# A selective-scan chunk loop on TensorE: own products head by head, one state addition, and another order of products, decay, rank, masks and scatters

## The chip, the cores and the metric

The kernel runs on one core of a Trainium2 chip. The metric is the device time of one execution in microseconds (us). The five engines of the core run their own instruction streams: TensorE (PE: matrix products, its weight loads listed apart as PEld), VectorE (DVE), ScalarE (ACT), GpSimd (POOL) and SyncE (SP, which here only issues transfers). They wait for each other through semaphores, and an instruction that waits holds back everything behind it on its own engine.

## The reference, cut to what matters

Two blocks run one after the other. The first is a state-space scan (Mamba-2) over 4 batches of 8 heads, 768 positions, head width 32 and state width 16; the second is a mixture of experts with one expert per token (3072 tokens of width 256, 8 experts, hidden width 1024).

```python
# scan; x [4,8,768,32], a [4,8,768], B and C [4,8,768,16]
log_a = np.log(np.clip(a, 1e-06, 1.0))
for c in range(nc):                                   # chunks; the result does not depend on their length
    cum = np.cumsum(la, axis=-1)
    L = np.exp(cum[:, :, :, None] - cum[:, :, None, :]) * causal
    M = np.einsum('bhin,bhjn->bhij', Cc, Bc) * L
    y_intra = np.einsum('bhij,bhjd->bhid', M, xc)
    y_inter = np.einsum('bhin,bhnd->bhid', Cc, state) * np.exp(cum)[:, :, :, None]
    y[:, :, sl] = y_intra + y_inter
    Bx = np.einsum('bhjn,bhjd->bhjnd', Bc, xc) * np.exp(cum[:, :, -1:] - cum)[:, :, :, None, None]
    state = np.exp(np.sum(la, axis=-1))[:, :, None, None] * state + np.sum(Bx, axis=2)
# experts; x is y with the heads side by side, [3072,256]
logits = x @ w_gate
expert_idx = np.argmax(logits, axis=1)
gate_w = softmax(logits)[np.arange(N), expert_idx]
out[mask] = gate_w[mask, None] * (np.maximum(x[mask] @ w1[e], 0.0) @ w2[e])      # mask: the tokens of expert e
```

Here `a` lies between 0.85 and 0.95, and all inputs are float32.

## The kernel before, in words

**The scan's steps.** A chunk is 64 positions (`CH`). The four batches make two pairs of 12 chunks (`NC`), so there are 24 steps (`NT`), steps 0 to 11 for the first pair and 12 to 23 for the second; chunk 0 of a pair has no state before it, and chunk 11 makes none. A step treats two batches (index t, on the two halves of the 128 partitions) and 8 heads, which are counted as head 4s + 2v + u with s, v, u of 0 or 1. Four chunks form a group (`CG`) whose inputs x, B and the transposed `BT` and `CT` are loaded together; there are six groups. The main loop over n (lines 801 to 884) stands under `tc.manual_schedule()`: every engine executes its instructions in the order in which this loop issues them. The loop is skewed: in turn n it treats the scores of step n, the state and the output of step k = n - 1, and the transposition of step j = k - 1.

**What one turn computes.** Nearly all products go through the helper `mm` (L176), so in the profile they are told apart by their tiles:

- `decay(n)` (L359) is a DVE scan that makes the triangle `L` of all 8 heads [128x512] from the row product `abc`.
- `fade(k)` multiplies the old state by its decay on ACT into `Sd`, two instructions. `own(k)` is the chunk's own contribution to the state, `A<-xn,bs` on PE: 8 matmuls of 64 columns, each for two heads u = 0, 1. A weight tile holds the scaled B of both heads (2 x 16 columns) and meets the x of both heads, so of each 32x64 result only the two diagonal 16x32 blocks are wanted. Partitions of u = 0 and of u = 1 alternate in sixteens, and `par` is the mask that tells them apart.
- `decay_in` computes the decay of step n + 2 on PE (`A<-adp,hsel`, three bf16 matmuls) into column block 1 of the same PSUM tile "A", and ACT copies it to `dec` (L339). `decayed_C(n+2)` multiplies `CT` by it on POOL into `ctd`.
- `state(k)` adds on DVE: new S = A x par + Sd, one instruction for u = 0 (L428 at chunk 0, L431 at the others) and one for u = 1.
- `y(k)` on PE: first `y<-ctd,S` (16 matmuls in the profile, 8 issued for two passes each), then `y<-M,xn` (32). ACT copies the result to `yT`.
- `scores(n)` on PE: `g<-ctm,bt`. `weigh(n)` on DVE (L386): `M` = g x L. `scaled_B(n)` on POOL makes `bs` = B x the last column of L, for the own products of the next turn. `a_rows(n+1)` on PE makes the next `abc`, one bf16 matmul of 512 columns.
- `masks(g+1, u)` (ACT, L293) makes `ctm`, a copy of `CT` times `par` for head u of each pair: half of the next group's per call, 128x512 elements, at the second and third chunk of a group.
- `rows(j)` (L463) transposes `yT` on PE and multiplies by the gate weights in one go (`rows_ps<-turn,yT`, 128x136 twice); ACT copies the rows [tokens x (256 + 8 logits)] into `rt`.

**Routing beside the scan.** Steps are put in row groups `RGS = [2, 3, 3, 3, 3, 3, 7]`. When a group's rows are there, `choose_max` and `choose` (DVE) find the expert, `count` (POOL) counts, `rank_pe` (PE, in a PSUM tile of its own under the tag "rows", so that it takes turns with `rows_ps`) and `rank` (DVE) give each token its place in its expert's list. For the first group these three stages fall 1, 2 and 3 turns after the group's last rows, for the others 1, 1 and 2. So turns 7, 10, 13, 16 and 19 choose, and turns 8, 11, 14, 17 and 20 rank. Then `place` (L553) writes the rows with an indirect DMA that POOL issues, one chunk per turn in turns 6 to 22: 17 in the scan; the last group's seven come later, inside the expert phase. Near the end of the scan come `empty` (turn 21), the loads `a_load` of the first two experts' rows (SP, after the last scatter), and in the last turn the transposition `xT_ps` (L632) with which the experts start.

**Loads.** Inputs of groups 2 to 5 and the first weights are sent by SP in batches of three. `mm` counts passes (two for float32, one for bf16), and a batch waits for the matmul at which the count reaches its mark:

```python
        passes[0] += 2 if rhs.dtype == FP32 else 1
        if batches and passes[0] >= 99 + 253 * sent[0] // 2:
```

**Before the loop**, POOL waits for two small inputs, `ad` and `az` (the decays in two layouts), clips them (`az` at L234) and splits them into bf16 parts (`adp` three, `azp`). The second pair's part is prepared in turns 3 to 9; at turn 4 DVE makes the second scan of `adf` (`decay_rows`).

**The experts.** From 83.20 us on, `m_h` (first product, L685), `m_y` (second, L720) and `general` treat expert after expert. None of this is in the change.

The PSUM tiles of the scan are `g`, `y`, `A` and `rows` with one buffer each and `abc` with two. The profile's names drop buffer numbers; `xn` is the x of a group, `bt` is `BT`.

## Time and profile before

| | |
|---|---|
| Time, median of 3 runs | 271.02 us (268.24, 271.02, 273.14) |
| The profiled execution | 271.81 us, of which its span is 270.0 us |
| TensorE busy | 252.9 us (94%), 3044 matmuls; weight loads 213.7 us (79%) |
| VectorE busy | 110.7 us (41%) |
| ScalarE busy | 104.5 us (39%) |
| GpSimd busy | 87.0 us (32%) |
| DMA | 43.57 MB, mean 161 GB/s |
| Chain that ended last | PE 82%, DVE 5%, DMA 4%, issue 4%, POOL 2%, ACT 1% |
| Scan and start | 0 to 83.20 us |
| Experts | 83.20 to 259.80 us, TensorE busy 176.43 of 176.60 us |

The span is one execution as the hardware profiler saw it, from the first to the last instruction; the 1.8 us between it and the execution's time lie outside. Busy shares are averages over stages with different limits: the experts, which are two thirds of the span, are TensorE alone, while the scan keeps four engines at work. A line of the timeline gives the start in us, the busy time of the group, the engine, the line, the tiles (out<-in), shapes, the count, and in brackets the idle time before it and what ended it. "issue" is idle time in which the engine waited for nothing that the profile shows. Each float32 matmul that is issued appears as two.

### The profile page before, as it was taken

What the parts mean: (1) busy time and instruction counts of PE and PEld (TensorE: products, weight loads), DVE (VectorE), ACT (ScalarE), POOL (GpSimd) and SP (SyncE); (2) the same over time, 40 slices, a digit from 0 to 9 for tenths busy, and PEclk for the clock granted to TensorE, in tenths of its full rate; (3) what the DMA queues carried; (4) which work ended last, traced back from release to release, by engine and by line L of the source; (5) the groups of instructions that cost most, each with busy time, mean ns of one, the idle gap of its engine ahead of it and who ended that gap; (6) DMA issues with size and microseconds to landing.
All of it is one profiled execution on the core that took longest, in us unless ns stands there. A gap on an engine that the chain in (4) does not pass through costs nothing.

```text
span 270.0 us, 7603 instructions
## 1 busy us (share of the span) xinstructions
PE 252.9 (94%) x3044; PEld 213.7 (79%) x3067; DVE 110.7 (41%) x358; ACT 104.5 (39%) x304; POOL 87.0 (32%) x171
## 2 busy tenths in 40 slices
PE   8799898999997999999999999999999999999990
PEld 2577677677776888888888888888998978989770
DVE  4889887888854240421211111233225115321010
ACT  6958574655543423223232323141050520604200
POOL 5666875866720002025504120202211102121021
PEclk9999999999999999999999999999999999999996
DMA  6956767671434899949695959533330601401010
GB/s 182 374 172 171 228 199 236 165 247 51 135 118 101 212 367 310 384 177 294 236 256 202 279 199 335 130 91 78 103 85 9 94 4 30 90 6 40 2 35 28
DMA packets 29715, 43.57 MB, mean 161 GB/s; under 512 B 16203, under 2 KB 19917, under 8 KB 27984
## 3 DMA queue, kind: packets, MB, share of 16 engines
q1 hardware_dynamic: 27152, 36.32, 45.4%
q0 software_dynamic: 2496, 6.41, 7.1%
q8 instruction: 36, 0.59, 0.9%
q14 instruction: 31, 0.25, 0.3%
HBM read 29.10 MB, written 10.73 MB: 147 GB/s over the span
## 4 chain that ended last, share of the span: by engine, by line
PE 82%; DVE 5%; DMA 4%; issue 4%; POOL 2%; ACT 1%; POOLq 0%; ACTq 0%; DVEq 0%
PE h_ps L685 33%; PE y_ps L720 30%; PE y L176 5%; PE rows_ps L176 4%; PE g L176 3%; PE A L176 3%; PE yh_ps L731 3%; DVE L L359 2%; DMA x_hbm<-rows,pos 1%; DMA xs<-x_hbm 1%; DMA az<-in_az_dram 1%; DMA ct<-in_CT_dram 1%; DVE M L386 1%; PE rank L176 1%; DVE S L431 1%
## 5 line engine op out<-in xcount | busy, mean ns | idle before, releaser
L685 PE MATMUL h_ps<-xT,w 128*128 128x256 f32 (+3 forms) x516 | 90.3, 334 | 0.6 <-ACT xT L641 0.5
L685 PEld LDWEIGHTS h_ps<-xT,w 128*128 128x128 f32 x516 | 81.3, 190 | 8.2 <-ACT xT L641 0.7
L720 PE MATMUL y_ps<-w,hT 128*128 128x256 f32 x384 | 84.9, 380 | 0.0
L720 PEld LDWEIGHTS y_ps<-w,hT 128*128 128x128 f32 x384 | 72.6, 190 | 10.5 <-issue 0.8
L696 ACT ACTIVATE hT<-h_ps 128x256 f32<-128x256 f32 (+3 forms) x128 | 43.3, 339 | 60.8 <-PE h_ps L685 53.1
L711 POOL DMA_INDIRECT out_dram<-yo,xs x24 | 23.7, 988 | 91.1 <-ACT yo L703 64.7
L553 POOL DMA_INDIRECT x_hbm<-rows,pos x24 | 24.4, 1015 | 20.6 <-DMA x_hbm<-zrows 13.3
L359 DVE TENSOR_TENSOR_SCAN L<-abc,ident 128x512 f32<-128x512 f32 x24 | 29.1, 1213 | 0.0
L651 DVE COPY pl<-xs 128x256 uint16<-128x256 uint16 x44 | 10.4, 298 | 43.8 <-DMA xs<-x_hbm 43.7
L658 DVE COPY xT<-plT 128x512 uint16<-128x512 uint16 (+1 forms) x30 | 10.6, 415 | 33.6 <-DMA plT<-pl 27.8
L703 ACT ACTIVATE yo<-y_ps,gate 128x256 f32<-128x256 f32 x14 | 6.6, 474 | 39.4 <-PE y_ps L720 24.5
L386 DVE TENSOR_TENSOR M<-g,L 128x512 f32<-128x512 f32 x24 | 16.5, 687 | 5.6 <-PE g L176 5.1
L176 PE MATMUL rows_ps<-turn,yT 128*128 128x136 f32 x96 | 15.4, 283 | 3.5 <-issue 2.7
L705 DVE TENSOR_SCALAR yo<-y_ps,gate 128x256 f32<-128x256 f32 x10 | 4.8, 482 | 29.3 <-PE y_ps L720 29.3
L176 PE MATMUL g<-ctm,bt 32*64 32x128 f32 x384 | 16.3, 280 | 0.5 <-ACT ctm L293 0.4
L176 PEld LDWEIGHTS rows_ps<-turn,yT 128*128 128x128 f32 x96 | 14.5, 192 | 1.3 <-issue 0.4
L711 POOL DMA_INDIRECT out_dram<-yh,xh x4 | 3.9, 978 | 35.7 <-ACT yh L733 23.9
L470 ACT COPY rows<-rows_ps 128x264 f32<-128x264 f32 x24 | 9.1, 380 | 13.5 <-PE rows_ps L176 10.9
L176 PE MATMUL y<-M,xn 64*32 64x64 f32 x768 | 12.9, 223 | 1.2 <-issue 1.2
L457 ACT COPY yT<-y 128x256 f32<-128x256 f32 x24 | 8.9, 372 | 12.2 <-PE y L176 10.2
L176 PEld LDWEIGHTS g<-ctm,bt 32*64 32x64 f32 x384 | 10.4, 131 | 3.2 <-ACT ctm L293 0.9
L366 POOL TENSOR_TENSOR bs<-bn,L 128x128 f32<-128x128 f32 x22 | 9.0, 410 | 11.1 <-DVE L L359 10.0
(132 smaller groups left out, 203.3 us busy)
## 6 DMA issues: line engine op xcount, KB each, us to landing
w<-in_w_dram SPq DMA_DIRECT2D x13, 1024.0 KB
x_hbm<-zrows SPq DMA_DIRECT2D x8, 463.8 KB
xn<-in_x_dram SPq DMA_DIRECT2D x12, 256.0 KB
w<-in_w_dram SPq DMA_DIRECT2D x12, 256.0 KB
xs<-x_hbm SPq DMA_DIRECT2D x8, 265.0 KB
ct<-in_CT_dram SPq DMA_DIRECT2D x6, 256.0 KB
bt<-in_BT_dram SPq DMA_DIRECT2D x6, 256.0 KB
bn<-in_B_dram SPq DMA_DIRECT2D x6, 256.0 KB
```

The lines of the kernel that those rows point to most:

```text
L176: i = nc.tensor.matmul(out, lhsT=lhsT, rhs=rhs, **kw)
L359: nc.vector.tensor_tensor_scan(out=s["L"].rearrange("p h i -> p (h i)"), data0=s["abc"], data1=ident8.rearrange("p h i -> p (h i)"), initi ...
L366: nc.gpsimd.tensor_tensor(out=bs[n % 2], in0=gr[n // CG]["B"][:, n % CG].rearrange("p (h m) -> p h m", h=8), in1=bc(st[n]["L"][:, :, CH - ...
L386: nc.vector.tensor_tensor(out=s["M"].rearrange("p (s v u) i -> p s v (u i)", s=2, v=2), in0=s["g"][:, :, 0:256].rearrange("p v (s f) -> p ...
L470: nc.scalar.copy(out=rt[g][:, k - R0[g], 0:DM + E], in_=p)
L553: s_ = nc.gpsimd.indirect_dma_start(out=x_hbm[:, :], out_offset=bass.IndirectOffsetOnAxis(ap=pos[:, k:k + 1], axis=0), in_=rt[grp[k]][:, k ...
L651: nc.vector.tensor_copy(pl[:, i, :, t], f[:, :, HB * t:HB * t + 128])
L658: nc.vector.tensor_copy(xT.bitcast(U16).rearrange("p t (j c) -> p c t j", c=2), tt)
L685: nc.tensor.matmul(p[:, i:min(i + step, n)], lhsT=w[:, c:c + 128], rhs=xT[:, t, i:min(i + step, n)], start=(t == 0), stop=(t == KT - 1))
L696: nc.scalar.activation(hT[:, f, 0:n], p, func=ACT.Relu)
L711: s_ = nc.gpsimd.indirect_dma_start(out=out[:, :], out_offset=bass.IndirectOffsetOnAxis(ap=xs[:, TOK:TOK + 1].bitcast(I32), axis=0), in_=y ...
L720: nc.tensor.matmul(p, lhsT=hT[:, f], rhs=w_sb[e][1][:, f * DM:f * DM + DM], start=(f == 0), stop=(f == FT - 1))
```

## The change

It edits the scan only. The parts, in the order of the code:

1. `own(k)` goes head by head: 16 matmuls of 32 columns in place of 8 of 64. The weight tile `bs` becomes twice as wide, [128, 4, 4, 16], where each pair of heads has the four blocks (B of u = 0, zero, zero, B of u = 1); two POOL memsets at the start write the zeros, and `scaled_B` writes the blocks 0 and 3. Head u's x meets the blocks 2u and 2u + 1, and the two heads add up in one 32x32 result without cross terms.
2. `state(k)` needs no mask: one DVE addition over all 128 columns (a copy at chunk 0).
3. `y(k)` issues `y<-M,xn` first and `y<-ctd,S` second.
4. `decay_in` for step n + 2 moves from behind `own` to behind the scores, `a_rows` and `weigh`, just ahead of `rows`, and writes columns 128 to 256 of the tile "y", not of "A". `decayed_C` comes a turn later, at the start of the turn.
5. `rank_pe` writes into columns 128 and up of "A" and comes behind `y`.
6. `choose_max` comes at the start of the turn; its subtraction runs on POOL (DVE for the last group), and the comparison `eq` moves into `choose`.
7. `masks` for groups from 2 on are made in quarters (128x256 elements), one per turn in all four turns of a group; group 1's stay in halves.
8. `place` gets a wait: its indirect DMA may start only after the last score matmul of the same turn.
9. `rows` takes its PSUM tile from its caller; in the last turn that is still one under the tag "A".

On PE a turn was: own, decay, [rank], y from the state, y from M, scores, abc, rows. It becomes: own, y from M, y from the state, [rank], scores, abc, decay, rows.

```diff
@@ -83,3 +83,3 @@
     adp = [sm.tile([128, NP * 128], BF16, name=f"adp{i}") for i in range(3)]
-    bs = [sm.tile([128, 8, NS], FP32, name=f"bs{i}") for i in range(2)]
+    bs = [sm.tile([128, 4, 4, NS], FP32, name=f"bs{i}") for i in range(2)]
 
...
@@ -292,3 +293,4 @@
         for u in uu:
-            nc.scalar.mul(m[:, :, :, u, :], gr[g]["CT"].rearrange("p (c s i) -> p c s i", c=CG, s=2), par[:, u:u + 1])
+            nc.scalar.mul(m[:, cc, :, u, :], gr[g]["CT"].rearrange("p (c s i) -> p c s i", c=CG, s=2)[:, cc],
+                          par[:, u:u + 1])
 
...
@@ -325,5 +327,11 @@
         if "A" not in st[k]:
-            st[k]["A"] = ps.tile([128, 2, 128], FP32, name="A", bufs=1)
+            st[k]["A"] = ps.tile([128, 256], FP32, name="A", bufs=1)
         return st[k]["A"]
 
+    def rank_bank(k):
+        return state_bank(k)[:, 128:128 + (RG + 1) * E].rearrange("p (n e) -> p n e", e=E)
+
+    def rows_bank():
+        return ps.tile([128, DM + E], FP32, name="rows_ps", tag="rows", bufs=1)
+
     def decay_in(ns, bank):
...
@@ -365,4 +373,9 @@
             return
-        nc.gpsimd.tensor_tensor(out=bs[n % 2], in0=gr[n // CG]["B"][:, n % CG].rearrange("p (h m) -> p h m", h=8),
-                                in1=bc(st[n]["L"][:, :, CH - 1:CH], [128, 8, NS]), op=ALU.mult)
+
+        nc.gpsimd.tensor_tensor(out=bs[n % 2][:, :, 0:4:3],
+                                in0=gr[n // CG]["B"][:, n % CG].rearrange("p (w u m) -> p w u m", w=4, u=2),
+                                in1=bc(st[n]["L"][:, :, CH - 1:CH], [128, 8, NS]).rearrange("p (w u) m -> p w u m", u=2),
+                                op=ALU.mult)
+
+    scored = [None]
 
...
@@ -397,12 +410,12 @@
         xk = gr[k // CG]["x"][:, k % CG]
-
         for s in range(2):
-            for t in range(2):
-                for v in range(2):
-                    r = slice(64 * t, 64 * t + 64)
-                    h = 4 * s + 2 * v
-                    mm(A[32 * (2 * t + v):32 * (2 * t + v) + 32, 0, 64 * s:64 * s + 64],
-                                     lhsT=bs[k % 2][r, h:h + 2].rearrange("p u m -> p (u m)"),
-                                     rhs=xk[r, h * D:(h + 2) * D], start=(s == 0), stop=(s == 1),
-                                     skip_group_check=True)
+            for u in range(2):
+                for t in range(2):
+                    for v in range(2):
+                        r = slice(64 * t, 64 * t + 64)
+                        o = (4 * s + 2 * v + u) * D
+                        mm(A[32 * (2 * t + v):32 * (2 * t + v) + 32, 64 * s + D * u:64 * s + D * u + D],
+                                         lhsT=bs[k % 2][r, 2 * s + v, 2 * u:2 * u + 2].rearrange("p b m -> p (b m)"),
+                                         rhs=xk[r, o:o + D], start=(s == u == 0), stop=(s == u == 1),
+                                         skip_group_check=True)
 
...
@@ -423,11 +436,7 @@
         new = wk.tile([128, 2, 2 * D], FP32, name="S", bufs=3)
-        A = st[k]["A"][:, 0].rearrange("p (s d) -> p s d", s=2)
-        for u in range(2):
-            d = slice(D * u, D * u + D)
-            if c == 0:
-                nc.vector.tensor_scalar(out=new[:, :, d], in0=A[:, :, d], scalar1=par[:, u:u + 1], scalar2=None,
-                                        op0=ALU.mult)
-            else:
-                nc.vector.scalar_tensor_tensor(out=new[:, :, d], in0=A[:, :, d], scalar=par[:, u:u + 1],
-                                               in1=st[k]["Sd"][:, :, d], op0=ALU.mult, op1=ALU.add)
+        A = st[k]["A"][:, 0:128].rearrange("p (s d) -> p s d", s=2)
+        if c == 0:
+            nc.vector.tensor_copy(new, A)
+        else:
+            nc.vector.tensor_tensor(out=new, in0=A, in1=st[k]["Sd"], op=ALU.add)
         carry[k + 1] = new
...
@@ -435,5 +444,14 @@
     def y(k):
-        p = ps.tile([128, 2, 512], FP32, name="y", bufs=1)
+
+        p = st[k]["y"] = ps.tile([128, 2, 512], FP32, name="y", bufs=1)
         inter = k % NC > 0
         xk = gr[k // CG]["x"][:, k % CG]
+        for s in range(2):
+            for q in range(4):
+                for t in range(2):
+                    r = slice(64 * t, 64 * t + 64)
+                    o = (4 * s + q) * D
+                    mm(p[D * q:D * q + D, t, s * CH:s * CH + CH], lhsT=xk[r, o:o + D],
+                                     rhs=st[k]["M"][r, 4 * s + q], start=(s == 0), stop=not inter,
+                                     skip_group_check=True)
         if inter:
...
@@ -445,12 +463,4 @@
                         mm(p[64 * v:64 * v + 64, t, s * CH:s * CH + CH], lhsT=carry[k][r, s],
-                                         rhs=st[k]["ctd"][r, o:o + CH], start=(s == 0), stop=False,
+                                         rhs=st[k]["ctd"][r, o:o + CH], start=False, stop=True,
                                          skip_group_check=True)
-        for s in range(2):
-            for q in range(4):
-                for t in range(2):
-                    r = slice(64 * t, 64 * t + 64)
-                    o = (4 * s + q) * D
-                    mm(p[D * q:D * q + D, t, s * CH:s * CH + CH], lhsT=xk[r, o:o + D],
-                                     rhs=st[k]["M"][r, 4 * s + q], start=(not inter and s == 0), stop=True,
-                                     skip_group_check=True)
         st[k]["yT"] = wk.tile([128, 2, 128], FP32, name="yT")
...
@@ -478,6 +487,5 @@
 
-    def choose_max(g):
+    def choose_max(g, eng=nc.gpsimd):
         n = RGS[g]
         lg = rt[g][:, :, 128:HB]
-        sh = [128, n, E]
         mx = route.tile([128, RG], FP32, name="mx")[:, 0:n]
...
@@ -485,8 +493,4 @@
         sub = route.tile([128, RG, E], FP32, name="sub")[:, 0:n]
-        nc.vector.tensor_tensor(out=sub, in0=lg, in1=bc(mx[:, :, None], sh), op=ALU.subtract)
-
-        eq = route.tile([128, RG, E], FP32, name="eq")[:, 0:n]
-        nc.vector.scalar_tensor_tensor(out=eq, in0=sub, scalar=0.0, in1=bc(rev_e[:, None, :], sh),
-                                       op0=ALU.is_equal, op1=ALU.mult)
-        rt_v[g] = eq
+        eng.tensor_tensor(out=sub, in0=lg, in1=bc(mx[:, :, None], [128, n, E]), op=ALU.subtract)
+        rt_v[g] = sub
 
...
@@ -495,3 +499,6 @@
         sl = slice(R0[g], R0[g] + n)
-        eq = rt_v[g]
+
+        eq = route.tile([128, RG, E], FP32, name="eq")[:, 0:n]
+        nc.vector.scalar_tensor_tensor(out=eq, in0=rt_v[g], scalar=0.0, in1=bc(rev_e[:, None, :], [128, n, E]),
+                                       op0=ALU.is_equal, op1=ALU.mult)
         m2 = route.tile([128, RG], FP32, name="m2")[:, 0:n]
...
@@ -785,2 +793,4 @@
         nc.gpsimd.memset(d1, 0.0)
+        for t in bs:
+            nc.gpsimd.memset(t, 0.0)
         decay_ready(0, adt)
...
@@ -807,2 +817,7 @@
                 decay(n)
+                if n > 2 and n + 1 < NT:
+                    decayed_C([n + 1])
+            for stage, q in jobs:
+                if stage == 0:
+                    choose_max(q)
             if 0 <= k < NT:
...
@@ -810,12 +825,8 @@
                 own(k)
-                if n > 1 and n + 2 < NT:
-                    decay_in([n + 2], state_bank(k)[:, 1:2])
-                for stage, q in jobs:
-                    if stage == 2:
-                        rank_pe(q, ps.tile([128, RG + 1, E], FP32, name="rank", tag="rows", bufs=1))
                 state(k)
                 y(k)
+                for stage, q in jobs:
+                    if stage == 2:
+                        rank_pe(q, rank_bank(k))
             for stage, q in jobs:
-                if stage == 0:
-                    choose_max(q)
                 if stage == 1:
...
@@ -829,4 +840,2 @@
                 scaled_B(n)
-                if n > 1 and n + 2 < NT:
-                    decayed_C([n + 2])
                 if n + 1 < NT:
...
@@ -834,5 +843,10 @@
                 weigh(n)
+                if n > 1 and n + 2 < NT:
+                    decay_in([n + 2], st[k]["y"][:, 0:1, 128:256])
 
-                if c in (1, 2) and g + 1 < NG:
-                    masks(g + 1, (c - 1,))
+                if g + 1 < NG:
+                    if g == 0 and c in (1, 2):
+                        mask_jobs += [lambda g=g, u=c - 1: masks(g + 1, (u,))]
+                    if g:
+                        mask_jobs += [lambda g=g, u=c // 2, i=2 * (c % 2): masks(g + 1, (u,), slice(i, i + 2))]
                 if n in act_jobs:
...
@@ -841,2 +855,4 @@
                     empty_consts()
+                if mask_jobs:
+                    mask_jobs.pop(0)()
             if 0 <= j < NT:
...
@@ -844,3 +860,5 @@
                     keep_on()
-                rows(j, "A" if n == NT + 1 else "rows")
+                    rows(j, ps.tile([128, 512], FP32, name="last_ps", tag="A", bufs=1))
+                else:
+                    rows(j, rows_bank())
                 q = grp[j]
...
@@ -854,3 +872,3 @@
                     else:
-                        choose_max(q)
+                        choose_max(q, nc.vector)
                         choose(q)
...
@@ -873,3 +891,7 @@
             if todo:
-                place(todo.pop(0))
+
+                d = place(todo.pop(0))
+                tc.add_manual_dep(d.ins, scored[0].ins.name,
+                                  mybir.DependencyInfo(mybir.DependencyClass.Sync, mybir.DependencyReason.DATA),
+                                  reason="behind a step's scores")
             for stage, q in jobs:
```

## The prediction

> **What bounds the kernel now.** I read the table of stretches first, then the chain of waits in order of time, then the timelines of TensorE (PE) and GpSimd (POOL) side by side, then the list of waits.

> The stretches (start:end, length, then busy us and instructions of each engine) split the span:

> ```profile
> 12.68:24.85 12.17, 11.21 (x362) 8.82 (x356) 11.16 (x25) 7.83 (x25) 7.87 (x28) 1.00 0.58 185
> 24.85:74.95 50.10, 45.40 (x1394) 35.95 (x1399) 42.40 (x103) 29.54 (x87) 35.41 (x76) 1.00 0.60 181
> 74.95:83.20 8.25, 6.67 (x172) 5.24 (x168) 3.52 (x8) 3.49 (x10) 1.42 (x2) 1.00 0.42 121
> 83.20:259.80 176.60, 176.43 (x961) 156.32 (x962) 44.39 (x202) 53.39 (x160) 32.84 (x35) 1.00 0.53 155
> ```

> The experts (83.20 to 259.80) keep PE busy throughout and are not edited; only the scan can move. The stretches begin at the scores of steps 2, 6 and 22, so 20 steps take 62.27 us, 3.11 each. The end of the scan hangs on the last scatter, not on PE:

> ```profile
> 75.55 3.50 DMA x_hbm<-rows,pos
> 79.06 0.02 issue
> 79.07 2.96 DMA xs<-x_hbm
> 82.04 0.04 issue
> 82.08 0.67 PE xT_ps L632 x4
> ```

> The expert phase begins 6.53 us after that scatter starts; what counts is when step 22 is reached.

> One step of PE without a stall, and two scatters with the stalls behind them:

> ```profile
> 53.82 0.67 PE L176 MATMUL g<-ctm,bt 32*64 32x128 f32 x16
> 54.65 0.63 PE L176 MATMUL rows_ps<-turn,yT 128*128 128x136 f32 x4 [0.16 <-issue]
> 55.20 0.43 PE L176 MATMUL A<-xn,bs 64*32 64x64 f32 x16
> 55.56 0.34 PE L176 MATMUL A<-adp,hsel 128*128 128x128 bf16 x3
> 55.84 0.46 PE L176 MATMUL y<-ctd,S 32*64 32x64 f32 x16
> 56.23 0.45 PE L176 MATMUL y<-M,xn 64*32 64x64 f32 x32
> 56.61 0.67 PE L176 MATMUL g<-ctm,bt 32*64 32x128 f32 x16
> ...
> 26.75 1.22 POOL L553 DMA_INDIRECT x_hbm<-rows,pos  x1 [0.31 <-POOL az L234]
> 28.05 0.45 PE L176 MATMUL y<-M,xn 64*32 64x64 f32 x16 [0.42 <-issue]
> ...
> 42.88 1.03 POOL L553 DMA_INDIRECT x_hbm<-rows,pos  x1 [1.36 <-DVE M L386]
> 44.20 0.33 PE L176 MATMUL y<-M,xn 64*32 64x64 f32 x5 [0.49 <-issue]
> ```

> From start to next start: scores g and the row product abc 0.82, rows 0.56, own products A 0.36, decay 0.27, y from the state 0.39, y from M 0.38: 2.78 us. A step with a rank adds 0.34.

> The stalls have a rule. PE waits for "issue", that is for no semaphore, and goes on 1.30 us after the scatter's start (28.05 - 26.75) and 1.32 (44.20 - 42.88); 61.48 to 62.83 and 46.78 to 48.12 give 1.35 and 1.34. Where y from M starts 1.4 us or more after a scatter, as at 56.23 after the one at 54.47, nothing is lost. So during a scatter PE gets no instructions and lives on what it has queued. Over the 16 steps from 24.85 to 74.95 that cost 0.79, 0.21, 0.38, 0.86, 0.54, 0.23, 0.60, 0.10: 3.7 us. The other loss is rank behind a busy bank or a count, about 1.0.

> ```profile
> DVE M L386 <- PE g L176: 5.1, 11, 1.4
> DVE S L431 <- ACT dec L339: 2.8, 6, 0.8
> ```

> VectorE (DVE) waits for PE, so PE is the bound and DVE is close behind. The second line is the state addition waiting for a copy out of its own PSUM bank.

> [...] the three decay products span 0.34 with a mean of 0.222, so they stand 0.06 apart, yet the next kind starts 0.27 after the first, 0.15 after the last: 0.09 us for a change. [...] after 26.75 PE still ran the 16 + 16 matmuls of y with their weight loads, 64, before it starved. [...]

> **The change, part by part.** Let g be the start of a step's scores.

> *Order on PE.* Now there are six changes of tile form per step (rows, A, decay, y, y, g, abc). After: rows, A, y from M (64*32 both), y from the state, g (32*64 both), abc, decay: three. So y from the state falls from 0.39 to 0.30, decay from 0.27 to 0.18, and A loses its 0.15 tail.

> *A head by head.* 16 matmuls of 32 columns for 8 of 64. Four tiles run in parallel; a round of 64 columns takes 0.055 (0.21 for four), one of 32 should take 0.028 if loads hide: 8 x 0.028 + 0.03 = 0.26. If rounds stay at 0.055 it is 0.47. I take 0.26; the scatter below hides the difference in 16 of 20 steps. New sum: 0.82 + 0.18 + 0.56 + 0.26 + 0.38 + 0.30 = 2.50.

> *Scatter behind the scores.* Now it starts anywhere. After, it needs the last score (g + 0.67) and about 0.15 of issue: g + 0.82, each time. PE is fed again at g + 0.82 + 1.32 = 2.14. By then it has done abc, decay and rows (to 1.56) and[...] nearly all of A, whose instructions double to 64. So y from M starts at 2.17 at best instead of 1.82. Refilling is slow: after 28.05 the 8 remaining matmuls took 0.017 each, so y takes 16 x 0.017 + 0.15 = 0.42. Step: 2.17 + 0.42 + 0.30 = 2.88, that is 0.38 lost per scatter. Now it is 3.7/16 = 0.23. On POOL, counts and the next ctd and bs queue behind the waiting scatter, which ends at g + 1.9 (2.8 with counts); bs needs the next L, ready about g + 2.55, so nobody waits.

> *One state addition, decay into y's bank.* Two DVE instructions of 273 ns become one of 128 columns, some 0.33; next starts after 0.25 instead of 0.37. S no longer waits for dec (2.8 us of DVE idle). DVE per step: M 0.60, L 1.13, S 0.25, then 0.71 in a choosing and 0.30 in a rank step, 6 of each in 20: 2.29. Below 2.88, so these gains are covered by PE.

> *Rank in A's bank, behind y.* Rank now waits until DVE has read S. S follows L and the fades on ScalarE (ACT). There the decay copy (g + 1.22), a mask quarter (1.47), the rows copy (1.77) and two fades (to 2.63) run in line; S goes from 2.7 to 3.0, rank starts at 3.08 instead of 2.97, plus 0.37: 3.45 per rank step. If ACT is not in the way, 3.34; if S slips by a choosing step's full 0.7, about 4.1.

> *sub to POOL, eq into choose.* The trip costs about 0.1 of DVE waiting in a choosing step, inside M's slack (M is done at g + 1.50, PE wants it at 2.17). *Masks in quarters* move 0.72 pieces into 0.38 ones; ct must be in one step earlier; group 2's was issued at 10.71 and is read near 18. *Loads* follow counted passes, 88 per step now, 104 after, so SP's batches come 18% sooner in steps; nothing waits for them, cost nothing, 0.5 once if one delays PE as at 14.8. *Two memsets of bs*, 0.3 each, sit before POOL's ad clip, which waits 0.45 for its DMA, with 1.87 idle later: nothing.

> **Sum.** Steps 7 to 22: 9 ordinary x 2.88 = 25.9; 5 rank x 3.45 = 17.3; steps 12 and 13, without A or without y from the state, 2.62 + 2.59 = 5.2. Together 48.4 against 50.1: -1.7. Steps 3 to 6 have no scatter but a late rank behind the second scan of adf: 3 x 2.5 + 4.1 + 0.45 (the stall at 14.8 kept) = 12.05 against 12.17: -0.1. Start: y from M no longer stands behind ctd: -0.1. Last scatter: g + 0.82 against 75.55 - 74.95 = 0.60: +0.2. Total -1.7: span 268.3. The profiled execution took 271.81, so 270.1; it lies 0.8 above the median of 271.02, so I predict 269.3.

> **Rivals.**
> *The scatter is covered (faster).* If the full-size products carry PE through[...], ordinary steps are 2.50: 9 x 2.5 + 4.4 + 5 x 3.56 (rank then waits for S longer) = 44.7, -5.4, the early steps -0.6, the end +0.2: -5.8, 265.2. For it: the scatters at 54.47 and 57.53, near a step's start, cost nothing. Against: PE goes on at start + 1.3 in every stalled step, and the product right behind rows is now the densest.
> *The starved stretch is longer (slower).* The block falls in front of 128 instructions (A and y from M). If PE holds few of A's when it begins, A also runs at 0.017 after it: +0.26 a step, 16 times: +4.2, 273.5. It decides from 0.11 per step (1.7/16). Against: PE spends 0.7 us in ten or so instructions before A[...].
> *Rank late.* S held up by 0.6 in each of six rank steps: +3.6, 272.9. For it: five engines' queues meet there.

> **How the numbers follow.** My forecast 0.64, own range 267.3 to 271.5. Covered 0.20, of which 0.16 beyond the mark of 2% (about what a measurement of this kernel can tell from no change: 265.6 and 276.4). Starved longer 0.11, rank late 0.05; of these two 0.03 and of the forecast's own upper tail 0.02 end beyond +2%. Faster 0.17, same 0.78, slower 0.05. The range 264.8 to 273.6 takes in both outer cases.

> **What would show it.** Right: PE's step starts near 2.9 apart; a PE gap marked issue at A or y from M, ending 1.3 after each scatter; y from the state to g 0.30; a wait of PE's rank for S. Wrong: no issue gaps and steps of 2.5 (covered), A spread over 0.4 or more after the gap (starved), DVE waiting less than PE (DVE the bound).

## The result, and the profile after

The changed kernel took 283.13 us (median of four runs, 283.12 to 284.61) against 270.86 for the kernel before: ratio 1.049, interval 1.042 to 1.057. Slower by 12 us, where 269.3 with a range of 264.8 to 273.6 was forecast.

The stretches of the profiled execution (284.61 us, span 282.9), cut at the scores of steps 2, 6 and 22 and at the experts as in the prediction; columns as there, the last three being TensorE's granted clock, DMA share and GB/s:

```profile
12.46:29.00 16.54, 11.52 (x437) 8.96 (x433) 10.04 (x21) 8.66 (x28) 10.05 (x33) 1.00 0.60 188
29.00:86.04 57.04, 49.19 (x1637) 37.75 (x1640) 39.61 (x82) 30.05 (x95) 35.53 (x79) 0.94 0.50 151
86.04:96.27 10.23, 8.63 (x199) 6.74 (x195) 3.12 (x5) 3.49 (x10) 1.01 (x1) 0.83 0.27 73
96.27:282.90 186.63, 179.39 (x973) 158.81 (x973) 44.70 (x203) 53.42 (x160) 35.03 (x38) 0.99 0.52 149
```

The experts are as long as before (186.63 us to the end of the span; before, 83.20 to 270.00, 186.80). The scan has all of the loss: steps 2 to 6 take 16.54 us (12.17 before), steps 6 to 22 57.04 (50.10), the rest 10.23 (8.25). Two things in these lines are new: PE is busy for only 11.52 of the 16.54 us, and its clock is 0.94 and 0.83.

Where PE stands still longest, the list of waits (engine, tile, line, then releaser: us in total, times, longest) names no semaphore, and it shows VectorE waiting for PE far longer than before (14.0 us for the scores, 5.1 before):

```profile
PEld y L176 <- issue: 9.0, 11, 2.4
PE y L176 <- issue: 6.0, 6, 2.2
DVE M L399 <- PE g L176: 14.0, 16, 2.2
```

The longest of these gaps, at step 4, in PE's timeline:

```profile
20.92 0.68 PE L176 MATMUL rows_ps<-turn,yT 128*128 128x136 f32 x4
21.53 0.46 PE L176 MATMUL A<-xn,bs 64*32 64x32 f32 x32
21.81 0.33 PE L176 MATMUL y<-M,xn 64*32 64x64 f32 x9
24.34 0.37 PE L176 MATMUL y<-M,xn 64*32 64x64 f32 x20 [2.21 <-issue]
```

The chain of waits in order of time has another near the end of the scan, where the kernel before had only the landing of the last scatter on it:

```profile
83.80 0.35 PE y L176 x19
84.15 1.72 issue
85.87 0.38 PE y L176 x9
```

The gap at step 4 falls in the middle of one product, whose inputs were there, and the first scatter is issued only at 30.64 us. So it is not the stall that the prediction knew. What is there at that time is one packet on q8, the queue that the profile names "instruction", in the DMA view of 21.6 to 23.1 us:

```profile
q8 instruction: 1, 0.02, 5.5%
```

I took the 16 KB packets on q8 from the trace, and counted PE's records up to each stall of over 0.15 us that follows one: in the first line matmuls and weight loads alone, in the second also PE's semaphore instructions, which the trace has too:

```text
record of the stall   443    696    948   1202   2975   3229   3482   4240   4494   4748
with semaphores       449    705    961   1217   3009   3265   3521   4289   4545   4801
PE idle, us          1.48   0.43   2.21   0.89   0.47   0.36   0.36   0.30   1.72   0.91
16 KB packet ends   13.71  17.62  22.99  26.77  60.40  64.11  68.60  79.68  84.57  88.75
PE goes on          15.16  19.09  24.34  28.24  61.79  65.40  69.87  81.15  85.87  90.01
difference           1.45   1.47   1.36   1.46   1.39   1.28   1.27   1.47   1.29   1.26
```

The stalls stand exactly 256 instructions apart, or 7 or 3 times that (some 253 of a block are matmuls and weight loads), and each ends 1.26 to 1.47 us after a packet has landed. I read such a packet as PE's next 256 instructions, called a block from here on, and the stall as PE run dry at the edge of the one before; what a packet holds, the trace does not say. The ten stalls cost 9.1 us.

The profile counts the packets over the whole execution. Before, and then after:

```profile
q8 instruction: 36, 0.59, 0.9%
```

```profile
q8 instruction: 39, 0.64, 1.0%
```

Three packets more is all that the totals show of it.

### The profile page after: what moved, and what is told of

It reads as the page before. It is cut to its first block, busy times and chain, and to the rows that moved or that the text cites. A ratio compares the mean times of both kernels' runs of the same rounds, so it can differ in the third digit from the quotient of the medians.

```text
span 282.9 us, 8370 instructions
## 1 busy us (share of the span) xinstructions
PE 258.8 (91%) x3419; PEld 217.2 (77%) x3419; DVE 106.6 (38%) x330; ACT 105.4 (37%) x312; POOL 88.9 (31%) x179
## 4 chain that ended last, share of the span: by engine, by line
PE 82%; issue 5%; DVE 5%; DMA 2%; ACT 2%; POOL 1%; POOLq 0%; ACTq 0%; SPq 0%; DVEq 0%
PE h_ps L693 31%; PE y_ps L728 28%; PE y L176 6%; PE g L176 4%; PE rows_ps L176 3%; PE A L176 3%; PE yh_ps L739 3%; PE abc L176 2%; DMA bt<-in_BT_dram 2%; DVE L L367 1%; DMA az<-in_az_dram 1%; DVE M L399 1%; POOL out_dram L719 1%; DVE S L441 0%; ACT Sd L429 0%
## 5 line engine op out<-in xcount | busy, mean ns | idle before, releaser
L560 POOL DMA_INDIRECT x_hbm<-rows,pos x24 | 24.3, 1013 | 33.1 <-issue 14.8
L176 PE MATMUL g<-ctm,bt 32*64 32x128 f32 x384 | 18.6, 287 | 1.4 <-issue 1.3
L176 PE MATMUL rows_ps<-turn,yT 128*128 128x136 f32 x92 | 17.1, 313 | 1.5 <-DMA bt<-in_BT_dram 1.5
L176 PE MATMUL y<-M,xn 64*32 64x64 f32 x768 | 14.0, 229 | 4.8 <-issue 3.0
L176 PEld LDWEIGHTS rows_ps<-turn,yT 128*128 128x128 f32 x92 | 13.8, 208 | 1.8 <-issue 1.7
L176 PEld LDWEIGHTS g<-ctm,bt 32*64 32x64 f32 x384 | 12.2, 136 | 3.1 <-issue 1.8
L176 PEld LDWEIGHTS y<-M,xn 64*32 64x32 f32 x768 | 9.8, 107 | 6.2 <-issue 5.4
L176 PE MATMUL y<-ctd,S 32*64 32x64 f32 x352 | 10.8, 235 | 3.1 <-issue 3.0
```

What stands on the lines that cost most here:

```text
L176: i = nc.tensor.matmul(out, lhsT=lhsT, rhs=rhs, **kw)
L560: s_ = nc.gpsimd.indirect_dma_start(out=x_hbm[:, :], out_offset=bass.IndirectOffsetOnAxis(ap=pos[:, k:k + 1], axis=0), in_=rt[grp[k]][:, k ...
```

## The experiments

Ratios are to the kernel before in the same session; the bracket is the 95% interval. The first four kernels shared one session, the next four another, then four and three; each session ran on another chip.

### Own products back to eight

```diff
-            for u in range(2):
...
-                        mm(A[32 * (2 * t + v):32 * (2 * t + v) + 32, 64 * s + D * u:64 * s + D * u + D],
...
+                    mm(A[32 * (2 * t + v):32 * (2 * t + v) + 32, 64 * s:64 * s + 64],
...
-            nc.vector.tensor_tensor(out=new, in0=A, in1=st[k]["Sd"], op=ALU.add)
+        for u in range(2):
...
+                nc.vector.scalar_tensor_tensor(out=new[:, :, d], in0=A[:, :, d], scalar=par[:, u:u + 1],
+                                               in1=st[k]["Sd"][:, :, d], op0=ALU.mult, op1=ALU.add)
```

> The changed kernel with its own products as they were: 8 matmuls of 64 columns with the mask, and the two masked state instructions. All else is as changed. TensorE's instructions per step fall from 208 records (matmuls and weight loads) to 176. Theory 'instruction blocks': in the changed kernel PE runs dry at the edges of 16 KB instruction blocks (every 253 records; ten stalls, each ending 1.26 to 1.47 us after the block has landed, 9.1 us together)[...]. At 176 records a block lasts 3.6 us or more in place of 3.1, so most of those stalls[...] go: 268 to 272 us, under two stalls at block edges. Rival 'VectorE late' (sub on POOL, rank behind the state): 280 to 284, since none of that is touched and the state addition even becomes 0.12 us longer. Rival 'scatter behind the scores': 280 to 284.

Measured 1.023 (1.015 to 1.031). About half of the loss went, not nearly all. The direction is that of the instruction blocks; the size says that they are not alone. The granted clock of the profiled execution did not rise: 0.963, against 0.976 in the changed kernel's.

### The kernel before with its own products split

```diff
+            for u in range(2):
...
-                    mm(A[32 * (2 * t + v):32 * (2 * t + v) + 32, 0, 64 * s:64 * s + 64],
...
-                                     rhs=xk[r, h * D:(h + 2) * D], start=(s == 0), stop=(s == 1),
...
+                        mm(A[32 * (2 * t + v):32 * (2 * t + v) + 32, 0, 64 * s + D * u:64 * s + D * u + D],
...
+                                         rhs=xk[r, (h + u) * D:(h + u + 1) * D], start=(s == u == 0),
```

> The kernel before with each 64-column own product issued as two of 32 columns with the same weights; order, banks, state instructions and everything else as before. PE gets 32 more records per step (176 to 208) and next to no more columns. Theory 'instruction blocks': a block must then last 3.77 us at 3.11 us per step, which is close to the least that the changed kernel's trace shows from one block's entry to the next (1.1 + 1.0 + 1.3 = 3.4 us): stalls at block edges in a third to half of the blocks, 3 to 7 us slower than before, 274 to 278. Both rivals: 271 to 272, as neither VectorE nor the scatters are touched.

Measured 1.045 (1.038 to 1.052): 280.86 against 268.57 us. Eight more matmuls per step in the old order, with nothing else edited, cost 12 us, as much as the whole change and more than I had expected. VectorE's work, POOL's, banks and scatters are those of before, so neither rival of the first run can say this. Nor is it array time. At step 18, without a stall, the own products take 0.39 us to the next product's start (0.36 before) and the step 2.81 (2.79 before):

```profile
68.14 0.67 PE L176 MATMUL g<-ctm,bt 32*64 32x128 f32 x16
69.52 0.46 PE L176 MATMUL A<-xn,bs 64*32 64x32 f32 x32
69.91 0.34 PE L176 MATMUL A<-adp,hsel 128*128 128x128 bf16 x3
70.95 0.67 PE L176 MATMUL g<-ctm,bt 32*64 32x128 f32 x16
```

One of its ten stalls at block edges (5.7 us together) cuts the own products two matmul records short of their end:

```profile
50.99 0.45 PE L176 MATMUL A<-xn,bs 64*32 64x32 f32 x30 [0.24 <-POOL bs L366]
52.45 0.25 PE L176 MATMUL A<-xn,bs 64*32 64x32 f32 x2 [1.01 <-issue]
```

The traced execution is the fastest of the four, 278.48 us, 9.9 above the kernel before. Beside the 5.7 us at edges, PE's clock was halved for 3.4 us; the rest is not taken apart.

In the trace of the kernel before, run again in the third session, no stall of PE ends 1.2 to 1.6 us after a packet on q8: there, counted in the same way, each block of the scan had landed 1.3 to 3.5 us ahead of its edge. In the changed kernel's first trace that was 1.26 to 1.99 us at all 18 edges.

The split also brings the loads sooner, since they follow counted passes, 104 a step. They can't be all of it either. While the block for the stall at 65.40 was on its way, from 61.8 to 65.4 us in the changed kernel's first trace, there was no load on the queues, only a scatter and the block:

```profile
q0 software_dynamic: 46, 0.14, 10.3%
q8 instruction: 1, 0.02, 2.1%
```

### The scatter's wait taken out

```diff
-                tc.add_manual_dep(d.ins, scored[0].ins.name,
-                                  mybir.DependencyInfo(mybir.DependencyClass.Sync, mybir.DependencyReason.DATA),
-                                  reason="behind a step's scores")
```

> The changed kernel without the wait of each scatter for the last score product of its step; all else as changed. Theory 'instruction blocks': the scatters hardly matter, 281 to 285. Rival 'scatter behind the scores' (it holds up the POOL queue, and PE behind it): 272 to 278. The prediction's own rule, that PE goes without instructions until 1.3 us after a scatter's start: stalls of 0.2 to 0.8 us at y from M come back, 283 to 287.

Measured 1.049 (1.042 to 1.056), as the changed kernel. The wait for the scores is not the cause. No stall came back 1.3 us after a scatter either, so my scatter rule failed too; more on that below.

### The subtraction on VectorE

```diff
-    def choose_max(g, eng=nc.gpsimd):
+    def choose_max(g, eng=nc.vector):
```

> The changed kernel with the subtraction of the choosing stage on VectorE as before, in place of POOL. Theory 'instruction blocks': the two worst choosing steps (53.8 and 45.1 us in the trace, where VectorE waits up to 1.5 us for POOL's subtraction) get 0.3 to 1 us shorter and one stretch of half clock may go: 279 to 283. Rival 'VectorE late': this is the main loss, 272 to 276.

Measured 1.041 (1.033 to 1.050), beside 1.049 for the run without the wait, its neighbour of the same session. The intervals overlap, so the gain is not certain. What it is about shows in the changed kernel at step 13, VectorE first and then PE:

```profile
54.49 0.38 DVE L502 SCALAR_TENSOR_TENSOR eq<-sub,rev_e 128x24 f32<-128x24 f32 x1 [1.48 <-POOL sub L494]
```

```profile
54.87 0.45 PE L176 MATMUL A<-xn,bs 64*32 64x32 f32 x32 [1.10 <-POOL bs L375]
56.05 0.46 PE L176 MATMUL y<-M,xn 64*32 64x64 f32 x32 [0.72 <-DVE M L399]
57.27 0.17 PE L176 MATMUL A<-cnt,ones_bf 128*128 128x24 bf16 x1 [0.37 <-DVE S L441]
```

POOL had a scatter (52.75 to 53.78) and `ctd` ahead of `sub`, and `bs` behind it; `eq` waits for `sub`, M for `choose`, and PE for all of it.

### Both causes away, one at a time

The next four have rank in the bank of the rows again, and vary the subtraction, the scatter's wait and the number of own products.

```diff
-                        rank_pe(q, rank_bank(k))
+                        rank_pe(q, ps.tile([128, RG + 1, E], FP32, name="rank", tag="rows", bufs=1))
```

> The changed kernel with own products and state instructions as before (as in the first run), the subtraction on VectorE, and rank in the bank of the rows again, at its new place behind y. What stays of the change is PE's order, the decay in y's bank, the scatter behind the scores and the masks in quarters. Theory 'two causes and a multiplier' (the instruction blocks; what the choosing and ranking steps wait for, namely POOL's subtraction and the state[...]): both causes are away[...], and the gains of PE's order are left: 265 to 269, no slower than before. Rival 'PE's order or the scatter is itself bad': 273 to 278 as in the first run.

Measured 1.012 (1.009 to 1.015). Better by a percent than the first run, but across sessions, and still slower than before, where 265 to 269 us was expected: what is left of the change has no gain.

The next leaves the subtraction on POOL:

> As the kernel sent with it, but the subtraction stays on POOL. Theory: the subtraction costs a stall of 1 to 1.8 us at step 13 (behind the scatter on POOL) and 0.4 in other choosing steps, and half a stretch of half clock: 269 to 273. If the state in front of rank is all: 265 to 269, as with the subtraction moved. If rank is nothing: 276 to 279.

Measured 1.012 (1.007 to 1.017), 275.58 us, which lies in none of the three forecasts: where rank is out of the way, it does not matter where the subtraction runs.

> As the first of these with the scatter's wait for the scores taken out as well. Theory: the scatter has nothing to do with it, within 1 us of its sibling. The prediction's scatter rule: stalls of PE that end 1.3 us after a scatter come back, 1 to 3 us slower. If the wait holds POOL up and with it the scaled B (step 13): 1 to 2 us faster.

Measured 1.018 (1.010 to 1.025): no gain from taking the wait out here either.

> The changed kernel with own products head by head kept, but the subtraction on VectorE and rank in the bank of the rows, behind y. Theory: only the instruction blocks are left as a cause, 9 us of stalls and one or two stretches of half clock: 275 to 280. If the waits of rank and choose are the main cause: 266 to 270.

Measured 1.040 (1.029 to 1.051), in the session in which its sibling with eight products has 1.012: the 16 products cost some 2 to 3%, not sharply, as its four runs spread from 279.52 to 284.35 us. Its trace has three starved edges, 3.8 us, against two, 2.4, in the sibling's, so here the edges are not the whole price.

### Both kernels again in one session

> The kernel before once more, unchanged, for its trace beside that of the changed kernel in the same session. In its first trace PE stood without instructions until 1.3 us after five of the scatters; in the first session's four kernels no PE stall ended 1.3 us after a scatter, in the second session's four most did. If the scatter rule belongs to the session (the chip or its memory), it holds here for both kernels or for neither; if it belongs to rank's bank (that of the rows in the kernels that showed it), it holds here for this kernel and not for the changed one.

> The changed kernel once more, unchanged. Theory 'instruction blocks': again stalls at multiples of 253 records, each 1.26 to 1.5 us after the block has landed, 282 to 285 us. The scatter rule as said for the kernel before.

271.51 and 284.35 us. Stalls at block edges again in the second (seven, 4.6 us), none in the first. In the third session the scatter rule held for both kernels (in the second, after the scatter at 70.40, PE goes on at 71.70, idle 0.43); in the changed kernel's first trace it held nowhere. The same step 18 of the same kernel, first trace and this one:

```profile
74.10 0.45 PE L176 MATMUL A<-xn,bs 64*32 64x32 f32 x32
74.37 0.53 PE L176 MATMUL y<-M,xn 64*32 64x64 f32 x32
74.84 0.38 PE L176 MATMUL y<-ctd,S 32*64 32x64 f32 x9
```

```profile
73.92 0.46 PE L176 MATMUL A<-xn,bs 64*32 64x32 f32 x32
74.19 0.89 PE L176 MATMUL y<-M,xn 64*32 64x64 f32 x32
75.02 0.38 PE L176 MATMUL y<-ctd,S 32*64 32x64 f32 x9
```

With the scatter at 1.04 us after the step's scores in both, y from M takes 0.47 in one and 0.83 in the other, and the step 2.57 and 2.94. So that PE is fed again only 1.3 us after a scatter's start is a matter of the session or its chip, not of the code. That is all that the runs say of it. The total hardly moved (283 and 284): where steps are longer, the blocks come in time more often (seven starved edges in place of ten).

### Rank behind the state, alone

This is the first run's kernel with the subtraction's edit of the fourth.

> The changed kernel with own products and state as before and the subtraction on VectorE; rank stays behind the state in A's bank. If rank's bank decides over the scatter stalls: no stalls 1.3 us after a scatter and ordinary steps of 2.5 us, 272 to 276 us (rank's waits for S cost 0.4 to 1.1 us six times). If the session decides, its steps are like those of the sibling kernel with rank in the rows' bank.

Measured 1.020 (1.017 to 1.024). The stalls behind scatters were there with rank in A's bank too, so it is the session or its chip. Rank's waits for S in its trace: 1.33, 0.63, 0.53 and 0.29 us. What rank's bank costs in time no pair of runs in one session isolates.

### Scatters earlier

```diff
+                early = bool(todo) and not any(stage == 2 for stage, q in jobs)
+                if early:
+                    d = place(todo.pop(0))
+                    tc.add_manual_dep(d.ins, first[0].ins.name,
...
                 scaled_B(n)
```

> Own products, state, subtraction and rank's bank as in the fifth run, and the scatters of steps without a rank earlier: ahead of the scaled B on POOL, behind the step's first score product, so about 0.9 us earlier in PE's step. By the scatter rule PE is fed again at 1.4 us after the step's scores begin, while it still works on the rows: ordinary steps of 2.55 to 2.6 us in place of 2.8 to 3.2, 3 to 5 us faster than the fifth run, 0.99 to 1.00 of the kernel before. If the scatter rule is wrong: as the fifth run, 1.01.

Measured 1.019 (1.016 to 1.021), a miss. The scatter started 0.77 us after the scores began, not at 0.1, and `bs` came behind it:

```profile
67.58 0.37 PE L176 MATMUL A<-xn,bs 64*32 64x64 f32 x12 [0.55 <-POOL bs L375]
```

One wait for another, at 0.55 us in most steps.

### What was left open, and the price once more

```diff
-                if n == 12:
+                if n == 20:
                     empty_consts()
```

> As the fifth run (own products, state, subtraction and rank's bank as before), with the zero rows made at turn 20 in place of 12, where no masks are made. If they are what makes step 13 long (5.2 us, of which 1.3 are waits of PE for the scaled B and M): step 13 near 4 us, 1.0 to 1.5 us faster than the fifth run, 1.006 to 1.009 of the kernel before. If step 13 is long for another reason: 1.01 to 1.014.

Measured 1.020 (1.013 to 1.026). Step 13 came down to 3.10 us, but step 12 went up to 3.94, with a block-edge stall of 1.43 in it. There were no stalls behind scatters in the last session, ordinary steps took 2.47 to 2.58 us, and PE outran the blocks even with eight own products: seven stalls at edges, 6.4 us.

```diff
+                if early:
+                    place(todo.pop(0))
                 scaled_B(n)
...
-            if todo:
+            if todo and not early:
```

> As the one before, and scatters of steps without a rank are issued ahead of the scaled B with no wait for the scores (the twelfth run had a wait for the first score and held up the scaled B). POOL is free at about 0.1 us before the scores begin, so the scatter should end at 0.9 us after their start, the scaled B at 1.4 and PE's supply come back at 1.2 us, in front of the own products at 1.56. Scatter rule: ordinary steps of 2.55 to 2.65 us, 3 to 5 us faster than the one before, 0.99 to 1.00. If the supply is then missed in the scores or the decay: no gain.

Measured 1.018 (1.009 to 1.026): no gain. In these runs there were no stalls behind scatters to win back, and the earlier scatters held up `bs`, for which PE now waits (us in total, times, longest):

```profile
PE A L176 <- POOL bs L375: 5.6, 7, 2.2
```

The last takes the own products and the state addition from the changed kernel again:

> As the one before, with the own products head by head and the single state addition again: 32 more PE records per step, nothing else. Theory 'instruction blocks': stalls at multiples of 253 records and perhaps half clock, 6 to 10 us slower than its sibling. If the count of instructions were harmless: within 1 us of it, or a little faster through the single addition.

Measured 1.045 (1.038 to 1.052): 280.83 against its sibling's 274.01. The 16 products, with their state addition, cost 6.8 us; it has 39 packets on q8 and its sibling 37. No version tried beats the kernel before.

## Why the prediction was wrong, point by point

**The step that failed** is the own products' price. I took 0.26 us of array time per step, 0.47 at worst. The array time was right: from A to y from M is 0.27, its records starting in fours within 0.02, a four 0.032 after the one before (0.028 forecast). But the 16 matmuls are 32 more records, 208 a step in place of 176, and I weighed these only against what PE runs on during a scatter, never against the supply of blocks, though I had the packets on q8 and counted passes for the loads. At 2.5 us a step, a block of 253 records is used up in 253/208 x 2.5 = 3.0 us. In the changed kernel's first trace, the blocks that PE had to wait for came 3.6 to 6.7 us after the one before, 4.1 in the middle (the first, in the start, left out). At 4.1 a record costs 16 ns, 32 of them 0.52 us a step, and 22 steps 11 us. That is an estimate from the late blocks alone; the split kernel measured 12, of which its trace shows 5.7 of 9.9 at the edges. Before, a block lasted 253/176 x 3.11 = 4.5 us, by the same estimate just enough: the bound beside PE was then the supply of its instructions, and I read "PE busy" as array time. The stall at 14.8, which I carried along as one that a load delays, was a block edge (record 439, 1.45 us after a packet).

**How the loss adds up.** Of the 13.1 us that the first trace's scan is longer, 9.1 stand idle at block edges. Waits for S, `bs` and M in choosing and ranking steps are 1.6 + 2.4 = 4.0. And PE's clock was halved three times for 3.4 us (granted 0.51 in 37.30:40.80, in 57.80:61.30 and in 91.90:95.40), 10 us in all, which can cost 5 at most; the second, with what came before it:

```profile
54.87:57.27 2.40, 1.31 (x81) 1.09 (x81) 2.27 (x5) 0.25 (x1) 2.10 (x6) 1.00 0.32 57
57.50:61.00 3.50, 3.50 (x70) 2.61 (x71) 2.18 (x4) 1.10 (x4) 1.72 (x4) 0.55 0.47 166
```

Idle in nearly half of 2.4 us, then half clock from 57.83 to 61.24. Each of the three stretches follows stalls: 1.02 us for S before the first, 1.10 for `bs`, 0.72 for M and 0.37 for S before this one, 0.91 at a block edge before the third. But after the longest stall, 2.21 us up to 24.34, the clock stayed at 1.00 until 37.35. That the stalls caused the half clock was my reading of this order; what halves it, no run isolates. Edges, waits and half clock sum to at most 18; up to 5 of it the shorter order must have paid back, which is the balance and not a measurement.

**PE's order.** The 0.09 us for a change of tile form was an estimate from the decay products alone. The order was right where nothing else stood in the way: y from the state 0.28 (0.30 forecast), decay 0.17 (0.18), a step without stalls 2.57 (2.50). With 16 own products the gain could not be had, since a faster step only uses up its block sooner; in the last session that held with eight, too.

**The scatter.** In the third session, which had the rule, the changed kernel's ordinary steps took 2.94 to 2.97 (2.88 forecast), in its first trace 2.57. So the covered rival was right for the step of one trace and the forecast for that of another, and neither for the time. That PE gets no instructions during a scatter and lives on what it has queued was my reading of the gaps. From a scatter's start to its stall PE ran 65 matmuls and loads at 26.75, 77 at 42.88, 33 at 46.78 and 66 at 61.48 in the first trace before: no fixed number is shown.

**Rank.** Intervals with a rank: 4.66, 4.18, 5.81, 3.50 and 3.63 against 3.45. The last two are the forecast; the first three pay the waits above. **sub to POOL**, costed at nothing within M's slack, kept VectorE waiting for 1.48 us at step 13, behind a scatter: I had counted the trip, not the queue. With it on VectorE that step took 4.84 us, and 5.85 in the same session on POOL. **The state addition** took 0.29 (0.33 forecast) and was covered, as said; it no longer waits for `dec` (2.8 us before), but 5.4 us in total for `Sd`.

**The rivals.** "The starved stretch is longer" had the right sign and the wrong mechanism: I let a scatter starve PE, not the blocks themselves. In the second session, five steps with a stalling scatter were 0.02 to 0.17 us longer with 16 products than with eight, where that rival had 0.26. "Rank late" was right about the wait for S, 1.6 us in the first trace where it had 3.6, but that is the smaller part.

What stays open: after own products, rank and subtraction are put back, 1.2 to 2% remain. Where scatters stall PE, that is 0.3 to 0.4 a step; where they do not, the faster order meets the edges of the blocks. No run separates the two within one session. Nor is it shown what makes a block late: that for the gap at 24.34 came while loads took 90.9% of the DMA engines' time (21.6 to 23.1 us), that for 65.40 with no load at all.

## What to carry to other kernels

Count an engine's instructions as well as its time: a float32 matmul here leaves four records, and with 208 of them in a step of some 2.5 us TensorE stood still at ten of 18 block edges, whatever the array could do, while the kernel before, which in the third session's trace used up its blocks in 3.4 to 5.6 us, stood at none. "issue" gaps whole multiples of 256 instructions apart, each ending 1.1 to 1.6 us after a packet on the instruction queue, were the sign here; splitting a matmul in two without changing its columns was the test, and cost 12 us. Before packing small products more finely, ask whether the array or the instruction stream is short.
